# A Fourier mixing and low-rank MLP kernel: the row shift in two parts, one step moved by a loop step, other buffers for the last outputs

## The chip, the cores and the metric

The kernel runs on one core of one Trainium2 chip. A core has TensorE (matmuls, called PE in the profile; its weight loads are PEld), VectorE (DVE), ScalarE (ACT), GpSimd (POOL) and SyncE (SP), and 16 DMA engines. Each engine works through its own instructions in order; between engines, semaphores set the order. The metric is the time on the device in microseconds (us), from launch to end of one execution; lower is better.

## The reference

The input x is 8 batches of 3136 rows of 256 floats. A Fourier transform goes along the rows and along the columns, of which the real part is kept; then a low-rank mixing over the rows, and a two-layer perceptron over the columns:

```python
X = np.fft.fft(x, axis=1)
X = np.fft.fft(X, axis=2)
x = X.real.astype(np.float32)

xt = x.transpose(0, 2, 1)
h = xt @ U @ V                       # U: 3136 x 32, V: 32 x 3136
u = x + h.transpose(0, 2, 1)
ch = np.maximum(u @ w_ch1, 0.0) @ w_ch2   # 256 -> 1024 -> 256
return (u + ch).astype(np.float32)
```

## The kernel before

The 3136 rows are split as 49 x 64 (`N1`, `N2`), so that the transform along the rows becomes a small transform of 49, a turn of the layout, and a transform of 64 that is done as matmuls with a table `T`. By symmetry only 25 of the 49 lines (`NK1`) are needed. The low-rank step is folded in: the lower 64 partitions of `g` hold the turned data, the upper 64 hold the low-rank vector `te` spread over all 25 lines, and the upper half of `T` holds V.

The work has three stretches:

**The front** (to about 31 us), written out by hand: tables of sines are built, the weights folded, and batch 0 transformed alone. `x_round` runs the transform of 49 for some of the 32 columns of each quarter (`quarter_products`, line 227, into PSUM), and evacuates them into `zts[0]` (columns 0 to 15) or `zts[1]` (16 to 31). `quarter_rows` (line 229) then shifts rows: eight copies, two for each of four groups of 32 partitions, bring a `zts` tile into `g0`. For `zts[1]` (line 669) six are on VectorE and two on ScalarE; in the profile they are copies `g<-zt` of 32x800 or 31x800 at the helper lines 76 and 73. Then follow `te_single` (line 293: 50 matmuls at line 298, two copies of the result to `te` at 269 and 270, and a `spread` of `te` over `g`), and the first groups of `s3_steps`.

**The loop** (from line 821) goes over 4 pairs of batches, in chunks of 512 rows at most, and each chunk has four loop steps. A step runs `mlp1` of this chunk (line 383: four matmuls into the PSUM tile `hps`, evacuated at 385 by ScalarE as `hT`), `mlp2` of the chunk before (394 and 397), then what `plan` has placed at this step, and last `drain`, the output of finished rows. `plan` (line 780) writes the order out by step numbers: `place(steps, lo, hi)` spreads a list of steps evenly over the loop steps from lo to hi. The first pair has in its list:

- `turned_steps` of batch 1, steps 10 to 17: as in the front, eight matmul rounds with `copy_act` into `zt`, and after every second one a `quarter_rows` of eight VectorE copies of 32x400, the last of them in step 17;
- `te_single` of batch 1 at step 18, with `spread_pool`: three GpSimd copies (line 306) over the lines 0 to 8, 9 to 16, and 17 to 24;
- the thirteen groups of `s3_steps` of batch 1 (line 322: matmuls of `T` and `g`, evacuated into `q`), over steps 19 to 30, evacuated by `copy_dve`;
- `place_next`: the loads of the next pair in eight chunks, at intervals of 2.6 steps from step 8: a load on SyncE (`xa`, line 96) and a gather on GpSimd (`xb`, line 99); four steps later the fold on GpSimd (144); seven later the fold on VectorE (134 to 136); nine and ten later two groups of `s1_steps` (matmuls at 185, evacuated by ScalarE into `z`).

`teps`, `tps` and `ps` of all these come in turn from one PSUM pool of two buffers (`psd`).

**The tail**: after the last chunk's `mlp1` steps, four calls of `mlp2` with `last` set are left. Each has a `drain` of its own: ScalarE copies half of the PSUM tile to `om` (406), VectorE adds and subtracts into `ob` (407, 408), and two DMAs store it (412). `ob` is from `opool`, which has four buffers, so a drain waits for the stores of the fourth drain before it.

Of the kernel before, what the change touches and what calls it, by code (L numbers as in the profile page):

```python
# [8 lines left out]
BF16 = mybir.dt.bfloat16  # L9
FP16 = mybir.dt.float16  # L10
FP32 = mybir.dt.float32
# [7 lines left out]
N1, N2, NK1 = 49, 64, 25  # L19
# [3 lines left out]
def kernel(  # L23
# [10 lines left out]
    B, S, D = x.shape  # L34
    R = moe_U.shape[1]
    H = moe_w_ch1.shape[1]
    P = 128
# [191 lines left out]
    def quarter_rows(g, zt, i0, engines):  # L229

        n = zt.shape[4]
        for q in range(4):
            d0 = 32 * q + i0
            for c in range(2):
                r = 32 - c
                engines[2 * q + c](g[32 * c:32 * c + r].rearrange("p k (s d) -> p k s d", s=2)[:, :, :, d0:d0 + n],
                                   zt[32 * q:32 * q + r, c])
# [55 lines left out]
    def te_single(pr, b, spread, ps=None):  # L293

        ps = ps or psd.tile([P, 2, D], FP32, tag="ps", name="teps")
        for k in range(NK1):
            for s, cs in enumerate([slice(0, 129), slice(129, 256)]):
                nc.tensor.matmul(ps[32 * s:32 * s + 32, 0, cs], us[:, k, s::2], pr.g[b][0:64, k, cs],  # L298
                                 start=(k == 0), stop=(k == NK1 - 1))
        te_out(pr, b, ps, 0, 32, spread)  # L300
# [13 lines left out]
    def s3_steps(pr, b, evac):  # L314

        if pr.q is None:
            pr.q = qpool[pr.p % 2].tile([P, 2, 6272], BF16, tag="q", name="q")

        def mm(o, k1, blk, st, rows=P, low=None):
            lt = low[:, blk::2] if low is not None else pr.g[b][0:rows, k1, blk::2]  # L320
            r = T[0:rows, k1, 0:64] if k1 == 0 else T[0:rows, k1, :].rearrange("p (s j) -> p s j", s=2)
            nc.tensor.matmul(o, lt, r, start=st, stop=True, skip_group_check=True)  # L322

        def lines(ps, g, blk, rows, low=None):
            for u in range(4):
                us = slice(u * 64, (u + 1) * 64)
                mm(ps[:, 0, us] if 4 * g + u == 0 else ps[:, :, us], 4 * g + u, blk, u == 0 and low is None, rows, low)

        def step(g, blk):
            ps = psd.tile([P, 2, 256], FP32, tag="ps", name="ps")  # L330
            lines(ps, g, blk, P)
            move(ps, g, blk, evac)

        def move_part(ps, g, blk, evac, part):
            lo = 64 if part and g == 0 else 0
            c0 = 3200 + b * 1536 + (4 * g - 1) * 64 if part else b * 1600 + 4 * g * 64
            evac(pr.q[:, blk, c0 + lo:c0 + 256], ps[:, part, lo:256])

        def move(ps, g, blk, evac):
            if g == 0:  # L340
                move_part(ps, g, blk, evac, 0)
                move_part(ps, g, blk, evac, 1)
            else:
                k0 = 4 * g
                evac(two(pr.q[:, blk, :], b * 1600 + k0 * 64, 3200 + b * 1536 + (k0 - 1) * 64, 256), ps[:])

        def last():
            ps = psd.tile([P, 2, 2, 64], FP32, tag="ps", name="ps")
            k1 = NK1 - 1
            for blk in range(2):  # L350
                mm(ps[:, blk], k1, blk, blk == 0)
            for blk in range(2):
                evac(two(pr.q[:, blk, :], b * 1600 + k1 * 64, 3200 + b * 1536 + (k1 - 1) * 64, 64), ps[:, blk])

        yield lines, move_part
        for g in range(6):
            for blk in range(2):
                yield lambda g=g, blk=blk: step(g, blk)
        yield last
# [27 lines left out]
    def mlp2(ch, t, last=False):  # L387
        q, nt = ch.pr.q, len(ch.units) // 2
        if t % 2 == 0 or last:
            ch.po = pso.tile([P, 2, 2, P], FP32, tag="o", name="ops")  # L390
        ps = ch.po[:, 0 if last else t % 2]
        tk = slice(ch.c0 + t * P, ch.c0 + (t + 1) * P)
        for j in range(JT):
            nc.tensor.matmul(ps, ch.h[:, j, t * P:(t + 1) * P], W2[:, j, :],  # L394
                             start=(j == 0 and (t % 2 == 0 or last)), stop=(j == JT - 1), skip_group_check=True)
            if j < 2:
                nc.tensor.matmul(ps[:, j], q[:, j, tk], (Bp if ch.sg > 0 else Bm)[:, j], start=False, stop=False,  # L397
                                 skip_group_check=True)
        if not (last or t % 2 == 1 or t == nt - 1):
            return lambda: None  # L400

        def drain():
            n = 1 if last else t % 2 + 1
            ob = opool.tile([P, 2, D], FP32, tag="ob", name="ob")
            om = opool.tile([P, 2, P], FP32, tag="om", bufs=2, name="om")
            nc.scalar.copy(om[:, 0:n], ch.po[:, 0:n, 1])  # L406
            nc.vector.tensor_tensor(ob[:, 0:n, 0:P], ch.po[:, 0:n, 0], om[:, 0:n], op=AL.add)  # L407
            nc.vector.tensor_tensor(ob[:, 0:n, P:D], ch.po[:, 0:n, 0], om[:, 0:n], op=AL.subtract)  # L408

            def store(i, hf, engine):  # L410
                b, r0 = ch.units[2 * (t - n + 1 + i) + hf]
                engine.dma_start(out=out[b].rearrange("(k2 k1) d -> k1 k2 d", k1=N1)[r0],  # L412
                                 in_=ob[hf * 64:(hf + 1) * 64, i])

            if not last or t == 0:
                for i in range(n):
                    for hf in range(2):
                        store(i, hf, nc.sync)
            else:
                store(0, 0, nc.sync)  # L420
                late.append(lambda: store(0, 1, nc.scalar))
            while last and late and (t == 1 or t == nt - 1):
                late.pop(0)()
        return drain
# [110 lines left out]
    def w2_fold(i):  # L535
        nc.vector.tensor_tensor(W2[:, :, i * P:(i + 1) * P], w2_f[:, :, 0], w2_f[:, :, 1],
                                op=(AL.subtract if i else AL.add))

    zts = [kpool.tile([P, 64 * NK1], BF16, name=f"zt{i}", tag=f"zt{i}").rearrange(
        "p (c k s i) -> p c k s i", c=2, k=NK1, s=2) for i in range(2)]  # L540
    g1 = gpool.tile([P, NK1, D], BF16, tag="g1", name="w2_f")
    w2_f = g1[:, 0:16].bitcast(FP32).rearrange("p (t s) d -> p t s d", s=2)

# [95 lines left out]
    def x_round(ps, i0, n):  # L639
        quarter_products(X0, ps, i0, n)  # L640

        def out(evac):
            j = i0 % 16
            evac(zts[i0 // 16][:, :, :, :, j:j + n].rearrange("p c k s i -> p s c k i"),
                 ps[:, :, :, :, 0:NK1].rearrange("p i s c k -> p s c k i"))
        return out

# [18 lines left out]
    outs = [x_round(round_view(bank_o("tps")), 24 + 4 * i, 4) for i in range(2)]  # L666
    outs[0](copy_act)
    outs[1](copy_act)
    quarter_rows(g0, zts[1], 16, [copy_dve] * 6 + [copy_act] * 2)
    nc.vector.tensor_copy(T[0:64, :, 64:128], T[0:64, :, 63::-1])  # L670

    teps = bank2("teps")
# [107 lines left out]
    def plan(p):  # L780

        at = [[] for _ in range(NS)]

        def place(steps, lo, hi):
            steps = list(steps)
            for i, s in enumerate(steps):
                at[lo + i * (hi - lo) // len(steps)].append(s)

        def place_next(nx, a, gap, s3lo):

            s1 = list(s1_steps(nx, copy_act))
            for c, (load, fn, fd) in enumerate(load_steps(nx)):
                for o, f in [(0, load), (4, fn), (7, fd), (9, s1[2 * c]), (10, s1[2 * c + 1])]:
                    at[int(a + gap * c) + o].append(f)
            e = int(a + gap * 7) + 11
            place([lambda: (turn(nx, 0, [(0, 8), (8, NK1)]), turn(nx, 1, whole))], e, e + 1)
            place(te_steps(nx, spread_pool), e, e + 2)
            place(list(s3_steps(nx, 0, copy_dve))[1:], s3lo, NS)

        cur = pairs[p]  # L800
        if p == 0:
            rest = []
            for t, f in zip([1, 2, 2, 3, 4, 5, 5, 6, 8], s3b0[4:]):
                at[t].append(f)
            at[0].append(lambda: w2_fold(0))
            at[2].append(lambda: w2_fold(1))
            place([late_tables], 8, 9)
            place([load_uz], 24, 25)
            place([lambda: rest.append(pair_tables())], 6, 7)
            place([lambda: rest[0]()], 10, 11)  # L810
            place(turned_steps(cur, 1, X1), 10, 18)
            place([lambda: te_single(cur, 1, spread_pool)], 18, 19)
            place(list(s3_steps(cur, 1, copy_dve))[1:], 19, 31)
            place_next(pairs[1], 8, 2.6, 44)
        else:
            place(list(s3_steps(cur, 1, copy_dve))[1:], 3, 18)
            if p + 1 < NP:
                place_next(pairs[p + 1], 0, 3.4, 40)
        return at
# [50 lines left out]
```

## The time and the profile before

Six runs gave a median of 451.67 us (450.75 to 453.93). The profiled execution took 454.93 us, with a span of 453.1 us from its first instruction to its last; the rest lies around it.

| what | us | share of the span |
|---|---|---|
| TensorE busy | 428.2 | 94% |
| ScalarE busy | 290.5 | 64% |
| VectorE busy | 226.0 | 50% |
| GpSimd busy | 142.9 | 32% |
| granted TensorE clock, mean | 0.990 of full | |

A row of the profile's tables reads: source line, engine, operation, output from input with their shapes, number of instructions, busy time, mean time of one, and then the idle time of that engine before it, with what ended the idle time behind the arrow. In the timeline, the first two numbers are the start and the length in us. A row of the windows shows a stretch, its length, the busy time of TensorE, its weight loads, VectorE, ScalarE and GpSimd with their number of instructions, then the granted clock, the busy share of the DMA engines, and GB/s.

### The profile page before, as it was taken

The numbers are of one execution on the slowest core, as the hardware profiler recorded it, in microseconds if no ns is written. First come the engines' busy times: TensorE is split into PE (matmuls) and PEld (weight loads), VectorE is DVE, ScalarE is ACT, GpSimd is POOL, SyncE is SP. The second block draws the span as 40 slices with busy tenths as digits, with TensorE's granted clock in tenths as the row PEclk, the third lists the DMA queues.
The fourth block names the chain that finished last, engine by engine and source line by source line (L and its number), as shares of the span: only waits on it lengthen the run. The fifth ranks groups of instructions, "written<-read, shape, count | busy, mean of one in ns | idle before, by whom it ended". The sixth has DMA issues, their size and how long they took to land.

```text
span 453.1 us, 10536 instructions
## 1 busy us (share of the span) xinstructions
PE 428.2 (94%) x4158; PEld 309.9 (68%) x4221; DVE 226.0 (50%) x541; ACT 290.5 (64%) x402; POOL 142.9 (32%) x180
## 2 busy tenths in 40 slices
PE   3699998999999999999999999999999999999995
PEld 1566665677867777767767777667767777677763
DVE  7674586766336367663354366663355345112212
ACT  5587754677465666777466666777465665666662
POOL 7445464951150544660420443660410000000000
PEclk9999998999999999999999999999999999999999
DMA  8749753785492538663682547763662222222323
GB/s 144 158 140 138 201 175 96 241 212 176 130 253 66 163 111 244 219 191 116 165 206 71 146 125 243 221 194 112 163 141 71 71 60 65 73 74 71 84 58 93
DMA packets 59761, 64.34 MB, mean 142 GB/s; under 512 B 12950, under 2 KB 52672, under 8 KB 59552
## 3 DMA queue, kind: packets, MB, share of 16 engines
q1 hardware_dynamic: 50000, 42.68, 35.9%
q0 software_dynamic: 7232, 14.30, 13.1%
q10 hardware_dynamic: 2480, 6.69, 3.9%
q8 instruction: 33, 0.54, 0.5%
q14 instruction: 16, 0.13, 0.1%
HBM read 34.62 MB, written 32.19 MB: 147 GB/s over the span
## 4 chain that ended last, share of the span: by engine, by line
PE 86%; DMA 4%; DVE 3%; issue 2%; SPq 1%; ACT 1%; POOL 1%; DVEq 0%; POOLq 0%
PE ops L394 36%; PE hps L383 35%; PE ps L322 5%; PE ops L397 5%; PE ps L185 3%; DMA X<-in_x_dram 2%; DMA out_dram<-ob 2%; PE tps L227 1%; DVE g L76 1%; PE teps L284 1%; SPq L412 1%; PE teps L298 1%; ACT hT L385 1%; DVE q L76 0%; DVE ob L407 0%
## 5 line engine op out<-in xcount | busy, mean ns | idle before, releaser
L385 ACT ACTIVATE hT<-hps 128x1024 bf16<-128x1024 f32 (+1 forms) x208 | 202.4, 975 | 111.0 <-PE hps L383 103.9
L394 PE MATMUL ops<-W,hT 128*128 128x256 bf16 x1568 | 225.2, 273 | 1.0 <-DVE ob L408 0.7
L394 PEld LDWEIGHTS <-hT 128*128 128x128 bf16 x1568 | 145.4, 98 | 35.3 <-DVE ob L408 0.8
L76 DVE CAST q<-ps 128x512 bf16<-128x512 f32 (+3 forms) x121 | 65.2, 559 | 85.7 <-PE ps L322 81.5
L383 PE MATMUL hps<-q,W1p 128*128 128x512 bf16 (+1 forms) x420 | 103.2, 355 | 2.3 <-DVE q L76 0.5
L407 DVE TENSOR_TENSOR ob<-ops,om 128x256 f32<-128x256 f32 (+1 forms) x102 | 41.8, 409 | 114.7 <-ACT om L406 113.9
L383 PE MATMUL hps<-q,W1m 128*128 128x512 bf16 x351 | 96.4, 381 | 2.2 <-ACT hT L385 0.5
L144 POOL TENSOR_TENSOR y<-xa,xb 98x510 f32<-98x510 f32 (+1 forms) x48 | 61.5, 1301 | 106.3 <-DMA xa<-in_x_dram 90.4
L383 PEld LDWEIGHTS <-W1p 128*128 128x128 bf16 x448 | 40.3, 97 | 26.9 <-issue 1.7
L383 PEld LDWEIGHTS <-W1m 128*128 128x128 bf16 x384 | 35.5, 98 | 26.9 <-issue 2.0
L397 PEld LDWEIGHTS <-q 128*128 128x128 bf16 x392 | 38.5, 98 | 21.5 <-issue 1.0
L406 ACT COPY om<-ops 128x256 f32<-128x256 f32 (+1 forms) x102 | 37.2, 365 | 12.5 <-PE ops L394 7.9
L306 POOL COPY g<-te 64x1024 int32<-64x1024 int32 (+1 forms) x23 | 24.8, 1120 | 60.9 <-DVE te L270 56.3
L408 DVE TENSOR_TENSOR ob<-ops,om 128x256 f32<-128x256 f32 (+1 forms) x102 | 41.0, 402 | 0.0
L73 ACT CAST z<-ps 128x512 bf16<-128x512 f32 x48 | 28.1, 585 | 17.9 <-PE ps L185 16.1
L397 PE MATMUL ops<-Bp,q 128*128 128x128 f16 x200 | 38.4, 219 | 0.0
L322 PE MATMUL ps<-T,g 128*128 128x128 bf16 (+3 forms) x400 | 36.9, 218 | 0.3 <-ACT q L73 0.3
L397 PE MATMUL ops<-Bm,q 128*128 128x128 f16 x192 | 37.1, 220 | 0.0
L322 PEld LDWEIGHTS <-g 128*128 128x128 bf16 (+1 forms) x400 | 29.5, 98 | 4.5 <-DVE q L76 0.4
L99 POOL DMA_INDIRECT xb<-in_x_dram,idx x24 | 24.4, 1018 | 5.4 <-issue 4.4
L76 DVE COPY g<-zt 32x400 bf16<-32x400 bf16 (+3 forms) x45 | 17.2, 382 | 8.7 <-ACT zt L73 8.1
L135 DVE TENSOR_TENSOR yb<-y 98x508 bf16<-98x508 f32 (+1 forms) x24 | 20.7, 862 | 0.0
(136 smaller groups left out, 211.3 us busy)
## 6 DMA issues: line engine op xcount, KB each, us to landing
out_dram<-ob SPq DMA_DIRECT2D x389, 64.0 KB
xa<-in_x_dram SPq DMA_DIRECT2D x24, 392.0 KB
zturn<-z ACTq DMA_DIRECT2D x9, 512.0 KB
g<-zturn SPq DMA_DIRECT2D x3, 800.0 KB
g<-zturn SPq DMA_DIRECT2D x3, 544.0 KB
X<-in_x_dram POOLq DMA_DIRECT2D x4, 384.0 KB, 8.5
X<-in_x_dram POOLq DMA_DIRECT2D x2, 744.0 KB
zturn<-z ACTq DMA_DIRECT2D x3, 448.0 KB
```

The lines of the kernel that those rows point to most:

```text
L73: nc.scalar.copy(o, i)
L76: nc.vector.tensor_copy(o, i)
L144: nc.gpsimd.tensor_tensor(ck.y[:, l0:l1, 1:256], ck.xa[:, l0:l1, 1:256], rb[:, l0:l1, 255:0:-1], op=AL.add)
L306: eng.tensor_copy(g[64:128, k0:k1].bitcast(I32), src.unsqueeze(1).to_broadcast([64, k1 - k0, D // 2]))
L322: nc.tensor.matmul(o, lt, r, start=st, stop=True, skip_group_check=True)
L383: nc.tensor.matmul(ps[:, i, 0:n], (W1p if ch.sg > 0 else W1m)[jp // 2][:, blk, j], q[:, blk, c0:c0 + n], start=(blk == 0), stop=(blk == 1))
L385: nc.scalar.activation(ch.h[:, 2 * jp:2 * jp + 2, 0:n], ps[:, :, 0:n], AF.Relu)
L394: nc.tensor.matmul(ps, ch.h[:, j, t * P:(t + 1) * P], W2[:, j, :], start=(j == 0 and (t % 2 == 0 or last)), stop=(j == JT - 1), skip_group ...
L397: nc.tensor.matmul(ps[:, j], q[:, j, tk], (Bp if ch.sg > 0 else Bm)[:, j], start=False, stop=False, skip_group_check=True)
L406: nc.scalar.copy(om[:, 0:n], ch.po[:, 0:n, 1])
L407: nc.vector.tensor_tensor(ob[:, 0:n, 0:P], ch.po[:, 0:n, 0], om[:, 0:n], op=AL.add)
L408: nc.vector.tensor_tensor(ob[:, 0:n, P:D], ch.po[:, 0:n, 0], om[:, 0:n], op=AL.subtract)
```

## The change

There are three edits. First, the second half of batch 0's columns gets two tiles of 8 columns each, `zts[1]` and `zts[2]`, in place of one of 16, and `quarter_rows` is called once for each, with six copies on VectorE and two on ScalarE each time. Second, in `plan`, `te_single` of batch 1 goes from step 18 to step 19, its thirteen groups of `s3_steps` go over steps 20 to 30, and these are evacuated by `copy_alt` (line 80), which alternates between ScalarE and VectorE. Third, `ob` of the last chunk's drains is taken from `xpool` under the tag `xa`, whose four buffers hold the input chunks earlier on.

```diff
         def drain():
             n = 1 if last else t % 2 + 1
-            ob = opool.tile([P, 2, D], FP32, tag="ob", name="ob")
+            ob = (xpool.tile([P, 2, D], FP32, tag="xa", name="ob") if last else
+                  opool.tile([P, 2, D], FP32, tag="ob", name="ob"))
...
-    zts = [kpool.tile([P, 64 * NK1], BF16, name=f"zt{i}", tag=f"zt{i}").rearrange(
-        "p (c k s i) -> p c k s i", c=2, k=NK1, s=2) for i in range(2)]
+    zts = [kpool.tile([P, 4 * n * NK1], BF16, name=f"zt{i}", tag=f"zt{i}").rearrange(
+        "p (c k s i) -> p c k s i", c=2, k=NK1, s=2) for i, n in enumerate([16, 8, 8])]
...
         def out(evac):
             j = i0 % 16
-            evac(zts[i0 // 16][:, :, :, :, j:j + n].rearrange("p c k s i -> p s c k i"),
+            zt = zts[0][:, :, :, :, j:j + n] if i0 < 16 else zts[i0 // 8 - 1][:, :, :, :, j % 8:j % 8 + n]
+            evac(zt.rearrange("p c k s i -> p s c k i"),
                  ps[:, :, :, :, 0:NK1].rearrange("p i s c k -> p s c k i"))
...
-    quarter_rows(g0, zts[1], 16, [copy_dve] * 6 + [copy_act] * 2)
+    for i in range(2):
+        quarter_rows(g0, zts[1 + i], 16 + 8 * i, [copy_dve] * 6 + [copy_act] * 2)
...
-            place([lambda: te_single(cur, 1, spread_pool)], 18, 19)
-            place(list(s3_steps(cur, 1, copy_dve))[1:], 19, 31)
+            place([lambda: te_single(cur, 1, spread_pool)], 19, 20)
+            place(list(s3_steps(cur, 1, copy_alt))[1:], 20, 31)
```

## The prediction

> **What bounds the kernel now.** I read the page's busy shares first, then the chain of waits, then what TensorE waited for, and last the timeline and the windows around the longest of those waits.
>
> ```profile
> PE 428.2 (94%) x4158; PEld 309.9 (68%) x4221; DVE 226.0 (50%) x541; ACT 290.5 (64%) x402; POOL 142.9 (32%) x180
> PE 86%; DMA 4%; DVE 3%; issue 2%; SPq 1%; ACT 1%; POOL 1%; DVEq 0%; POOLq 0%
> ```
>
> TensorE is busy 94% of the 453.1 us and carries 86% of the chain. So only what leaves TensorE idle or slow, or what comes after its last matmul, can move the time. The waits of TensorE between 20 and 100 us name the place:
>
> ```profile
> PE tps L227 <- issue: 2.9, 2, 2.5
> PE teps L298 <- DVE g L76: 1.5, 1, 1.5
> PE ps L185 <- DVE q L76: 0.6, 1, 0.6
> ```
>
> The columns are total us, times, longest. The second row is the low-rank step of batch 1 waiting for VectorE's last eight row copies. The timeline there:
>
> ```profile
> 70.91 1.27 POOL L144 TENSOR_TENSOR y<-xa,xb 98x510 f32<-98x510 f32 x1
> 71.13 3.04 DVE L76 COPY g<-zt 32x400 bf16<-32x400 bf16 x8 [0.90 <-ACT zt L73]
> ...
> 74.22 1.73 PE L298 MATMUL teps<-g,us 64*32 64x129 bf16 x50 [1.48 <-DVE g L76]
> ...
> 76.96 3.12 POOL L306 COPY g<-te 64x1152 int32<-64x1152 int32 x3 [4.60 <-issue]
> ```
>
> The copies end at 74.17; TensorE, done with its multilayer work at 72.74, stands 1.48. The windows show a second cost (the granted clock is the number before the DMA share):
>
> ```profile
> 72.00:74.00 2.00, 0.74 (x8) 0.41 (x5) 1.90 (x8) 0.81 (x1) 0.36 (x2) 1.00 0.39 98
> 74.00:76.00 2.00, 1.78 (x51) 1.58 (x52) 1.97 (x6) 0.00 (x0) 0.00 (x0) 0.88 0.03 8
> 76.00:78.00 2.00, 1.78 (x6) 0.77 (x7) 0.79 (x3) 0.59 (x1) 1.04 (x1) 0.50 0.13 33
> 78.00:80.00 2.00, 2.00 (x19) 1.58 (x17) 0.16 (x1) 1.02 (x1) 2.00 (x3) 0.76 0.46 115
> ```
>
> After the stall the clock falls to 0.50 until about 79.
>
> **Part 1, the first batch's row shift.** Six VectorE copies of 32x800 become twelve of 32x400; two ScalarE copies become four. VectorE stands still for 2.39 before 23.62, waiting for the last ScalarE copy of the transform. With own buffers its first six copies need only the first of those, begun at 21.71 and 0.83 long: they start at 22.56. Eight back-to-back copies of 32x400 took 2.12 at 66.08, so 0.265 each; twelve make 3.18 and end at 25.74, against 25.83 now. The table's median of 0.255 agrees; its mean of 0.38 holds the few copies that ran against a GpSimd fold, and GpSimd is idle from 22.07 to 28.24. TensorE ends its weight products (24.54 and 1.29) at 25.83 and starts the low-rank step at 25.89. So at most 0.06 is won.
>
> ScalarE pays. A 31x800 copy takes 0.855; half the elements take between half of it (0.43) and, by the 0.49 of a 128x400 evacuation, 0.52. Four make 1.7 to 2.1 against 1.72: 0 to 0.4 later. Behind them in ScalarE's queue stand two copies into T, W1p, Bp and the first q copies, which end at 30.29; the first hidden-layer matmul runs at 30.20, straight behind the second weight fold (29.18, 1.18 long), which hides most of the shift. I book 0 (from -0.06 to +0.4).
>
> **Part 2, the low-rank step a loop step later.** Removed from its place: 50 matmuls, two te copies on VectorE, three spread copies on GpSimd. In between now come the second matmul pair of chunk 0 (0.22) and one step of multilayer work (1.85, start to start, as at 436.17 to 438.02). TensorE: 72.74 + 0.22 + 1.85 = 74.81, later than 74.17, so the stall of 1.48 goes. The step's 50 matmuls took 1.59 at 25.89 near full clock, but the one here began before the clock fell and took 1.73: I use 1.5 to 1.6, ending at 76.4.
>
> The clock. From 75.88 to 79.34 the chunk pair and one step took 3.46, against 0.23 + 1.85 = 2.08 for the same at full clock (80.59 to 82.67): 1.38 lost. Here a rule speaks against me. The Trainium skill, TensorE: Matmul & The Clock Gate, HAM oscillation, says that idle gaps above some 3.4 us throttle the array; 1.48 is far less. By the rule alone the slow stretch is not the stall's and stays, so the part saves 1.5; by the row, where the only long stall of this stretch is followed by 0.50, it saves about 2.9. The same page's Part 1 calls the window free-running, so a short gap may or may not count. I take the row. Its 1.38 is the least certain term, since an unprofiled run may lie differently to the window.
>
> What is late next. The te copies follow the 50 matmuls; in the trace GpSimd starts its spread 1.01 after they end (75.95 to 76.96), so at about 77.4. Its first copy of three (3.12 / 3 = 1.04) ends at 78.4. TensorE, after the pair of chunk 1 (0.22) and another step (1.85), is at 78.4 to 78.5: a wait of 0 to 0.1.
>
> The queues that the move passes. On GpSimd the gather of chunk 4 (a DMA issue of 0.97) now stands before the spread. The order of the changed program shows that the spread's first copy also waits for that gather's landing, as it waits for the one of chunk 3 now. Free at 72.37, GpSimd issues it at about 72.4. Landings in the trace took 3.8 (issued 80.38, at a low DMA share) up to 7.9 (51, at a share of 0.71 to 0.90). At 72 to 76 the share is 0.39, then 0.03, so I take 3.8: 76.2, ahead of te. At 7.9 it is 80.3 and costs 2.9 (rival B). A second rule bears on it: the skill's SBUF — State Buffer, "SBUF: two separate sides", says that a VectorE copy in a two-port mode keeps GpSimd from writing a gather's descriptors. Then the landing counts from the copies' end: 74.2 + 3.8 = 78.0, and 0.6 is lost. The gather at 63.54 ran within such copies (60.76 to 65.37) in 0.97, the same as the median 0.96, so I go with 76.2. SyncE's order is unchanged; its load of chunk 4 already precedes. VectorE's te copies stay behind the stores' additions of the step before, which end at 76.22: no loss.
>
> The evacuations. Of batch 1's thirteen groups, about half move from VectorE to ScalarE. After the first two groups TensorE waits 0.59 for four VectorE copies in a row (79.84 to 81.12); with two engines I work out 0.45, since ScalarE reaches them only after the hidden layer's activation: 0.14 gained. Six copies of 512 columns (0.58) and two or three small ones load ScalarE by some 4 us between 78 and 106, on 23.97 busy of 34 (78 to 112): about 80%. Activations have two PSUM buffers and follow their matmuls by a step, so a delay of half a microsecond is covered; if not, 0.5. The thirteen groups now share eleven steps instead of twelve, but the first chunk that reads batch 1 (step 24) still finds its groups done by step 22.
>
> Sum: 1.48 + 1.38 + 0.14, and 0.1 back for the te matmuls at the better clock, less 0.1 for the spread: **3.0 saved**. TensorE stays busy (33.2 of 34 us from 78 to 112), so it passes to the end; SyncE's backlog behind the UZ load at 94.23 starts with stores that move along with TensorE.
>
> **Part 3, the last output buffers.** VectorE's last addition waits 0.47 for a store, and starts 0.60 after its ScalarE copy where the two before start after 0.30: 0.3 seems to be won. But the end hangs on SyncE:
>
> ```profile
> 441.81 8.78 SPq L412 DMA_DIRECT2D out_dram<-ob  x12
> L412 SPq DMA_DIRECT2D out_dram<-ob x1: 546/546/546, 450.0 to 450.0; - x1
> ```
>
> It issues stores without a pause from 445.0 to 450.55; the last data are ready at 449.44, the last store starts at 450.0. The 0.3 is hidden: 0 (from -0.3 to 0).
>
> **Sum and time.** The profiled run took 454.93 (span 453.1); less 3.0 it is 451.9. It stands 3.3 above the median of 451.67 (450.75 to 453.93), so I carry the difference: 451.67 - 3.0 = **448.7**.
>
> **The rivals.** 0.5% is 2.3 us, about what a measurement can tell from no change.
> - A, chance 0.60: as summed, 447.7 to 449.4.
> - C, 0.27: the stall goes but the slow clock was not in most runs, or comes anyway: 1.48 + 0.14 less 0.1 = 1.5, so 450.2 (449.4 to 450.9). For it: the other runs lie below the profiled one, and the rule above. Against: the windows.
> - B, 0.07, the other side: the gather of chunk 4 holds the spread. From a landing at 77.4 on, each microsecond is one of TensorE's. At 7.9 the spread starts at 80.3 and its first copy ends at 81.4: 2.9 idle, and if the clock falls again as it does now, 1.4 more. Net 3.0 - 4.3: 453.0, slower than before by 0.3%. It breaks even at about 6.6 from issue to landing. For it: two landings of 7.8 and 7.9. Against: the quiet DMA.
> - D, 0.06: ScalarE is too full, in front (0.4) and with thirteen groups (0.5 to 1), with small stalls that bring the slow clock (1.4): 450.4 to 453, and a tenth of it beyond.
>
> The range 447.6 to 451.6 leaves out the far parts of A, B and D. Faster by over 0.5% (under 449.4): A and a little of D, 0.62. Within: C, the middle of B and D, 0.33. Slower: the ends of B and D, 0.05.
>
> **What would show it.** Right: no wait of the 50 matmuls on the row copies, the clock at 1.00 from 72 to 80, the spread starting about a microsecond after the matmuls, the wait of 0.6 shortened, the low-rank step of batch 0 still at 25.9, SyncE still issuing to the end. Wrong: a wait of TensorE on the spread or of the spread on the gather, ScalarE copies ahead of a hidden-layer wait, or a low clock that stays.

## The result and the profile after

The changed kernel takes a median of **451.91 us** (449.6 to 453.77, 34 runs); the kernel before, beside it on the same chip, 452.73 (71 runs). The ratio is 0.998, with a 95% interval of 0.9967 to 0.9992: some 0.8 us faster, where 3.0 were forecast. A second comparison gave 0.9994 (0.9974 to 1.0014). No more than half a microsecond to one is there. Here and below, a ratio and its interval are worked out from all runs of both kernels, so a ratio need not equal the quotient of the two medians beside it.

The profiled execution took 451.8, with a span of 450.0. That is 3.1 less than the profiled execution before, and so very nearly the forecast. The median did not follow. Explaining this gap is most of what comes below.

The first two lines are the busy shares and the chain of waits of the kernel after:

```profile
PE 426.0 (95%) x4159; PEld 308.5 (69%) x4221; DVE 223.9 (50%) x539; ACT 294.4 (65%) x412; POOL 143.8 (32%) x180
PE 88%; DVE 6%; ACT 2%; issue 2%; POOL 0%; DVEq 0%; POOLq 0%; ACTq 0%
```

TensorE is busy 2.2 us less than before although it has the same work: it ran fewer microseconds at half clock. ScalarE has 3.9 us more, mostly the evacuations that it took over. Next, what TensorE waited for between 20 and 100 us (in total, times, longest):

```profile
PE teps L298 <- DVE g L76: 0.8, 1, 0.8
PE ps L185 <- DVE q L76: 0.7, 1, 0.7
...
PE ps L185 <- ACT q L73: 0.5, 1, 0.5
```

The first row looks like the old stall, halved. It isn't: its place is 23.93, in the front, where batch 0's low-rank step waits for the split row shift. The stall of batch 1 is gone, as the timeline from 68 to 78 shows:

```profile
69.38 3.23 DVE L76 COPY g<-zt 32x400 bf16<-32x400 bf16 x8 [0.91 <-ACT zt L73]
...
70.78 0.95 POOL L99 DMA_INDIRECT xb<-in_x_dram,idx  x1 [0.17 <-issue]
...
73.00 1.59 PE L298 MATMUL teps<-g,us 64*32 64x129 bf16 x50
...
75.42 3.12 POOL L306 COPY g<-te 64x1152 int32<-64x1152 int32 x3 [3.68 <-DVE te L270]
...
76.61 0.57 PE L322 MATMUL ps<-T,g 128*128 128x64 bf16 x8
...
77.02 0.65 ACT L73 CAST q<-ps 128x256 bf16<-128x256 f32 x2 [0.18 <-PE ps L322]
...
77.42 0.63 DVE L76 CAST q<-ps 128x192 bf16<-128x192 f32 x2 [0.82 <-ACT q L73]
...
77.83 0.38 PE L185 MATMUL ps<-yb,F 98*128 98x258 bf16 x2 [0.66 <-DVE q L76]
```

The copies end at 72.61, the 50 matmuls start at 73.00 with no idle time named before them, and the spread starts 0.83 after they end (74.59). The gather issued at 70.78 landed 3.9 later, ahead of `te`. The first two groups at 76.61 don't wait for the spread. In the last three rows a new order shows: ScalarE and VectorE evacuate the two groups, but one after the other (VectorE waits 0.82 for ScalarE), and TensorE waits 0.66. The windows show the clock (the number before the DMA share) at full speed:

```profile
72.00:74.00 2.00, 2.00 (x47) 1.72 (x47) 1.94 (x7) 1.02 (x1) 0.00 (x0) 1.00 0.62 193
74.00:76.00 2.00, 1.94 (x32) 1.37 (x28) 1.40 (x6) 1.05 (x3) 0.58 (x1) 1.00 0.13 34
76.00:78.00 2.00, 1.34 (x18) 1.04 (x16) 1.18 (x5) 1.49 (x3) 2.00 (x3) 1.00 0.37 93
```

To see where the 3.1 us of the two profiles came from, I set the hidden-layer activations (line 385) of both side by side, 208 in each, and took the difference of their starts, after less before:

| activation | start after less before, us | reading |
|---|---|---|
| first | -1.96 | the front of before's profile ran late, partly at half clock |
| 18th | -1.75 | nothing gained yet in the loop |
| 22nd | -5.08 | 3.3 gained around the low-rank step |
| 27th | -4.01 | 0.9 given back from the 25th (-4.93) on |
| 69th | -2.98 | 1.0 given back since the 68th (-4.01), near 175 us |
| end of span | -3.1 | |

So the step that was forecast to save 3.0 did save it in this pair of profiles (3.1, once a group of 0.22 is counted that after still owes there). But 2 us of the difference is the front, where the forecast had booked nothing, and 2 us were given back later.

The late front of before's profile comes and goes. TensorE waits there once for 2.5 before a run of transform matmuls (line 227), for nothing that the profile names: it is the longest wait of the first row in the prediction's list. This wait is 2.5 to 2.9 in five of the 17 profiles (before, the repeated change and three others) and at most 1.4 in the rest, and half clock begins near its end in those five alone. In the sixteen profiles that have it, TensorE goes on 2.3 to 2.8 after a 16-KB packet of the instruction queue (q8) starts, which is at 18.1 to 18.3 in the five and at 15.7 to 16.5 in the others. Why it starts later in some is open.

### The profile page after: what moved, and what is told of

Read it like the earlier page. It is cut to its first block, busy times and chain, and to the rows that moved or that the text cites. A ratio compares the mean times of both kernels' runs of the same rounds, so it can differ in the third digit from the quotient of the medians.

```text
span 450.0 us, 10537 instructions
## 1 busy us (share of the span) xinstructions
PE 426.0 (95%) x4159; PEld 308.5 (69%) x4221; DVE 223.9 (50%) x539; ACT 294.4 (65%) x412; POOL 143.8 (32%) x180
## 4 chain that ended last, share of the span: by engine, by line
PE 88%; DVE 6%; ACT 2%; issue 2%; POOL 0%; DVEq 0%; POOLq 0%; ACTq 0%
PE ops L394 37%; PE hps L383 35%; PE ps L322 5%; PE ops L397 5%; PE ps L185 3%; DVE g L76 2%; PE tps L227 2%; PE teps L284 1%; ACT hT L385 1%; PE teps L298 1%; DVE q L76 1%; DVE ta L448 0%; DVE yb L134 0%; DVE yb L135 0%; ACT q L73 0%
## 5 line engine op out<-in xcount | busy, mean ns | idle before, releaser
L76 DVE CAST q<-ps 128x512 bf16<-128x512 f32 (+3 forms) x113 | 60.8, 558 | 84.7 <-PE ps L322 79.4
L134 DVE TENSOR_TENSOR yb<-y 98x508 bf16<-98x508 f32 (+1 forms) x24 | 21.9, 912 | 0.1
L135 DVE TENSOR_TENSOR yb<-y 98x508 bf16<-98x508 f32 (+1 forms) x24 | 21.8, 910 | 0.0
```

The lines of the kernel that those rows point to most:

```text
L76: nc.vector.tensor_copy(o, i)
```

## The experiments

Two theories to begin with. **Stall and clock**: the stall and the half clock behind it are what the move wins, and something else takes most of it back. **Clock by chance**: the half clock is not the stall's, so only 1.5 was there to win. Later runs ask what takes it back: the front, the packing of thirteen groups in eleven steps, or the wait near 175 us.

### One part at a time

**Move alone**, with the evacuations left on VectorE:

```diff
-            place([lambda: te_single(cur, 1, spread_pool)], 18, 19)
-            place(list(s3_steps(cur, 1, copy_dve))[1:], 19, 31)
+            place([lambda: te_single(cur, 1, spread_pool)], 19, 20)
+            place(list(s3_steps(cur, 1, copy_dve))[1:], 20, 31)
```

> Only the low-rank step of batch 1 goes to step 19, its groups to steps 20 to 30, evacuated by VectorE alone as before. Theory A (the stall of 1.5 us goes in every run, but the half-clock stretch followed it only in some runs, and the other parts are nothing): the same 0.8 to 1.5 us under the kernel before as the whole change. Theory B (the move saves its 3.0 us in most runs, and the evacuations on ScalarE or the front give 2 us back): 2.5 to 3 us under.

451.38 against 452.63; ratio 0.9984 (0.996 to 1.0008): about what the whole change wins, within the noise. The stall is gone, and between 68 and 100 us TensorE waits four times for an evacuation: 0.6, 0.2, 0.5 and 0.6.

**Evacuations alone**, with the step left where it was:

```diff
-            place(list(s3_steps(cur, 1, copy_dve))[1:], 19, 31)
+            place(list(s3_steps(cur, 1, copy_alt))[1:], 19, 31)
```

> Only the evacuations of batch 1's groups alternate between ScalarE and VectorE; the low-rank step stays at step 18. Theory A: within 0.3 us of the kernel before. Theory B, if ScalarE is what gives back: 1 to 2 us slower.

452.92; ratio 1.0002 (0.998 to 1.0025): nothing. The wait after the first groups is 0.7, not shorter than 0.6. The stall of 1.5 is there, but in this profile no half clock follows it.

**Front alone**, the row shift in two parts:

```diff
-    quarter_rows(g0, zts[1], 16, [copy_dve] * 6 + [copy_act] * 2)
+    for i in range(2):
+        quarter_rows(g0, zts[1 + i], 16 + 8 * i, [copy_dve] * 6 + [copy_act] * 2)
```

> Only the row shift of batch 0 in two parts. Theory A: within 0.3 us, and the low-rank step of batch 0 starts as soon after its weight products as before. Theory B, if the front gives back: 1 to 2 us slower, seen as a wait of the low-rank step on the row copies.

452.95; ratio 1.0014 (0.9995 to 1.0034). Again the stall is there and no half clock. Here are the windows of this run, and below them those of the kernel before, profiled a second time in a later run (its label is e12_before_again):

```profile
68.00:70.00 2.00, 2.00 (x16) 1.20 (x14) 1.54 (x3) 2.00 (x4) 1.66 (x3) 1.00 0.59 203
70.00:72.00 2.00, 0.52 (x19) 0.48 (x20) 1.90 (x7) 0.11 (x1) 0.00 (x0) 1.00 0.24 64
72.00:74.00 2.00, 2.00 (x46) 1.51 (x41) 1.96 (x7) 0.53 (x1) 0.00 (x0) 1.00 0.04 8
```

```profile
70.00:72.00 2.00, 1.21 (x44) 1.22 (x46) 1.94 (x6) 0.00 (x0) 0.00 (x0) 1.00 0.11 30
72.00:74.00 2.00, 2.00 (x20) 0.99 (x15) 1.37 (x6) 0.59 (x1) 0.47 (x1) 0.60 0.02 4
74.00:76.00 2.00, 2.00 (x12) 1.34 (x11) 0.00 (x0) 1.02 (x1) 2.00 (x3) 0.54 0.41 107
```

The same stall, 1.48 of idle in each, and the clock drops behind one and not behind the other. Of the six profiles that have the stall (before twice, and four experiments) two show the drop.

What sets these two apart can be read from the traces. In all 17, the recorded changes of the clock lie whole multiples of 3.41 us apart (10.24, 51.2 and 61.44, for example), as if TensorE were judged in windows of this length; where they begin differs from one profile to the next. Here is the window that holds most of the stall, and what TensorE did in it beside the low-rank step's small matmuls:

| profile | window, us | other matmuls, us | clock in the next window |
|---|---|---|---|
| before | 72.12 to 75.53 | 0.62 | 0.50 |
| before, again | 69.00 to 72.41 | 0.33 | 0.50 |
| later pairs' evacuations (below) | 73.04 to 76.46 | 0.82 | 1.00 |
| front alone, again (below) | 72.83 to 76.24 | 0.97 | 1.00 |
| front alone | 68.38 to 71.79 | 1.66 | 1.00 |
| evacuations alone | 68.16 to 71.57 | 1.97 | 1.00 |

The clock drops where the stall and most of the 50 small matmuls (64 rows, 32 columns) fall into one window, and not where the window's edges part them or more of other work lies inside. These are six cases that came by chance, not a test; what a small matmul counts for they don't settle.

**Stall filled** with six matmuls of 512 columns, whose result is overwritten by the step's own, so that TensorE is busy while it waits:

```diff
+        for i in range(6):
+            nc.tensor.matmul(ps.rearrange("p a d -> p (a d)"), W2[:, 0, 0:P], W1p[0][:, 0],
+                             start=True, stop=True)
```

> The kernel before, with six extra matmuls of 128x512 (1.3 us at full clock) that fill TensorE while it waits for the last row copies of batch 1; their result is overwritten. The stall stays as long, but the clock has no reason to fall. Theory A: the half-clock stretch is there in some runs only, so the median falls by 0.5 us or less. Theory B: it is there in most runs, and the median falls by 1 to 1.4 us.

452.33; ratio 1.0006 (0.998 to 1.0032). The six take the place of the idle time, so what is left to win is the clock alone, and it can't be seen in the median. If each execution lost 1.38 to it, the ratio would be 0.997, outside the interval.

### How often the clock drops

The profiles are few, but every run records its mean granted clock. A stretch of 3.41 us at half clock lowers the mean over 452 us by 3.41 x 0.5 / 452 = 0.0038. Counting a mean below 0.9965 as one such stretch, below 0.9925 as two, below 0.9885 as three, gives what the traces of all 17 profiled executions show. Over all runs for which a clock is on record (the filled stall is among those without; ± is one standard error):

| kernels | runs | share with a stretch | stretches per run |
|---|---|---|---|
| with the stall, front as before | 282 | 49% | 0.61 ± 0.04 |
| with the stall, front split | 36 | 53% | 0.94 ± 0.19 |
| without the stall, front as before | 86 | 30% | 0.35 ± 0.06 |
| without the stall, front split | 115 | 52% | 0.68 ± 0.07 |

The stall brings 0.26 stretches a run, not one, and the split front brings 0.33. (Set against runs on the same chip alone, they bring 0.23 ± 0.08 and 0.34 ± 0.09.) Runs of the kernel before with no stretch average 451.73, with one 452.92: a stretch costs about 1.2. So the stall's clock is worth 0.26 x 1.2, some 0.3 us, and the split loses about 0.4 by the same sum.

### The thirteen groups

Packing thirteen groups in eleven steps pairs two of them at step 25 as well. The timeline of the kernel after:

```profile
89.08 0.61 PE L322 MATMUL ps<-T,g 128*128 128x128 bf16 x8
...
89.51 0.59 ACT L73 CAST q<-ps 128x512 bf16<-128x512 f32 x1 [0.18 <-PE ps L322]
...
90.14 0.38 PE L185 MATMUL ps<-yb,F 98*128 98x258 bf16 x2 [0.45 <-ACT q L73]
```

Eight matmuls back to back fill both buffers of the pool, and the next product waits 0.45 for an evacuation. Before had no such wait. Three runs change the packing: the change with the groups over twelve steps; the change with the pairs placed by hand; and that placement without the front split and the tail.

```diff
-            place(list(s3_steps(cur, 1, copy_alt))[1:], 20, 31)
+            place(list(s3_steps(cur, 1, copy_alt))[1:], 20, 32)
```

> The changed kernel, its thirteen groups of batch 1 over twelve steps (20 to 31) instead of eleven, so that only step 20 has two groups and no longer step 25. Theory A (the new waits of TensorE for evacuations, 0.66 us after the pair of step 20 and 0.45 us after the pair of step 25, eat what the stall gave): the wait of 0.45 us is gone from the trace, and the median lies 0.4 to 0.5 us under the changed kernel. Rival R (the folds of VectorE and GpSimd, which now fall together, slow everything behind them, whatever the places of the groups): no difference from the changed kernel.

```diff
-            place(list(s3_steps(cur, 1, copy_alt))[1:], 20, 31)
+            for t, f in zip([20, 21, 21, 22, 23, 24, 25, 26, 27, 28, 29, 30, 31],
+                            list(s3_steps(cur, 1, copy_alt))[1:]):
+                at[t].append(f)
```

> The changed kernel with the thirteen groups placed by hand at steps 20, 21, 21, 22, 23 and so on to 31: the one pair stands in step 21, where no transform matmuls of the next pair follow it. Theory A: both waits of TensorE for evacuations are gone, and the median lies 0.9 to 1.1 us under the changed kernel. Rival R: no difference.

> The changed kernel again, to be compared with the others on the same chip and to see a second profile of it. Theory A: 0.8 us under the kernel before; the waits for evacuations of about 0.7 and 0.5 us stand in its trace again, the one of 1.05 us near 175 us may not. Rival R: the wait near 175 us stands again.

> The kernel before with only the low-rank step at step 19 and the groups of batch 1 placed as in the last but one run, alternating between ScalarE and VectorE; the row shift of batch 0 and the last output buffers as before. Theory A (front and tail edits give nothing): as the run with both, within 0.3 us. If the front's edit costs: 0.3 us or more below it.

All against 452.34. Over twelve steps: 451.17, 0.9987 (0.9968 to 1.0005); the 0.45 is gone and 0.7 at step 20 stays. By hand: 451.46, 0.9988 (0.9972 to 1.0003); both are gone, but a wait of 0.9 on a VectorE evacuation takes their place. The change again: 452.59, 0.9994. By hand without the split and the tail: 450.72, 0.997 (0.9953 to 0.9987), in spite of the same 0.9. The two kernels placed by hand differ by 0.7 in the median; that points to the front, though they differ in the tail's buffers as well.

### The wait near 175 us, and a version that beats both

The repeated change shows what gave a microsecond back near 175 us:

```profile
174.01 3.20 POOL L144 TENSOR_TENSOR y<-xa,xb 98x510 f32<-98x510 f32 x2 [4.21 <-DMA xa<-in_x_dram]
...
174.32 1.76 DVE L135 TENSOR_TENSOR yb<-y 98x508 bf16<-98x508 f32 x1
...
176.00 1.25 DVE L136 CAST yb<-y 98x8 bf16<-98x8 f32 x1
...
177.81 1.27 DVE L76 CAST q<-ps 128x512 bf16<-128x512 f32 x2
...
178.54 0.38 PE L185 MATMUL ps<-yb,F 98*128 98x258 bf16 x2 [1.10 <-DVE q L76]
```

A fold on VectorE that takes 0.68 elsewhere takes 1.76 while GpSimd folds, and a copy of 8 columns 1.25 instead of 0.17. The evacuations queue behind them. Is this the change's? The kernel before, profiled again, answers: between 110 and 180 us it has the same wait.

```profile
PE ps L185 <- DVE q L76: 1.1, 1, 1.1
```

It comes and goes with where the folds meet. Before had it in one of two profiles, after in both, and the experiments in some: in six of all 13 profiles in which VectorE alone evacuates the later pairs. The next runs evacuate the later pairs' groups on both engines in turn, so that nothing queues behind a fold alone:

```diff
-            place(list(s3_steps(cur, 1, copy_dve))[1:], 3, 18)
+            place(list(s3_steps(cur, 1, copy_alt))[1:], 3, 18)
```

First it is put on top of the placement by hand, without split and tail, with that placement alone and the kernel before once more beside it:

> The kernel before with the low-rank step at step 19 and the groups of batch 1 placed without a pair ahead of transform matmuls, and in the later pairs the groups of the second batch evacuated by ScalarE and VectorE in turn instead of VectorE alone. Theory A2 (VectorE's folds, held up while GpSimd folds, delay the evacuations queued behind them, and TensorE waits 1.05 us for one near 175 us): that wait is gone or under 0.5 us, and the median is 0.3 to 1 us below the run with VectorE alone. Rival (that wait is chance and seldom): no difference, or slower by what ScalarE adds.

> The kernel before with only the low-rank step at step 19 and the groups of batch 1 placed without a pair, once more: 1.0 to 1.6 us under the kernel before if the first result holds. A2: a wait of TensorE of about 1 us for VectorE near 170 to 180 us stands in its trace again. Rival: it does not.

> The kernel before, for a second profile. Theory A (the half-clock stretch after the stall is rare, and the rest of its profiled run's excess lay in the front): the stall of 1.5 us stands, the clock stays full after it. Theory B: half clock for 3.4 us after the stall again. A2 as a part of the change: no wait of 1 us near 175 us here. Rival: one may stand here too.

449.06 against 451.82, ratio **0.9944** (0.9928 to 0.9959); without the later pairs' edit 450.19, 0.9973 (0.995 to 0.9995); before against itself 0.9998 (0.9982 to 1.0013). In the first of these, TensorE's only wait between 110 and 180 us is 0.2:

```profile
PE hps L383 <- ACT hT L385: 0.2, 1, 0.2
```

Then the same again with the front split, without it, the later pairs' edit alone, and the front split alone:

> The best version so far (low-rank step at step 19, no pair of groups ahead of transform matmuls, later pairs evacuated by ScalarE and VectorE in turn) with the row shift of batch 0 in two parts added. Theory F (the split costs in the front: more and longer copies there, and more half-clock windows): 0.4 to 0.6 us slower than the same kernel without the split, and a lower mean clock over its runs. Rival (the split is nothing): within 0.2 us.

> The best version once more, beside the one with the split on the same chip: 2 to 3 us under the kernel before if its first 7 runs hold; no wait of about 1 us near 175 us.

> The kernel before with only the later pairs' groups evacuated by ScalarE and VectorE in turn; the stall at the low-rank step of batch 1 stays. A2 (the wait of about 1 us near 175 us is in the kernel before too, in most runs): about 1 us under the kernel before. Rival (the wait came with the change): no difference.

> The kernel before with only the row shift of batch 0 in two parts, once more. Theory F: 0.4 to 0.6 us slower than the kernel before. Rival: within 0.2 us.

Against 453.39: with the split 450.91, 0.9944 (0.992 to 0.9968); without it **449.81, 0.9932** (0.9908 to 0.9956); the later pairs' edit alone 452.01, 0.9974 (0.9957 to 0.999); the split alone 453.98, 1.0027 (1.0001 to 1.0052). The version without the split, with the low-rank step at 19, the groups placed by hand and both engines evacuating all pairs, beats the kernel before in both of its comparisons; the change was not beside it there, but its ratios (0.998 and 0.9994) lie above both intervals. The 1.1 between the medians with and without the split fits the front's cost, though the intervals overlap. The wait near 175 us stands in none of the four profiles with the later pairs' edit. That accounts for some 0.5 on average (1.1 in six of 13), while the edit alone won 1.2; what else it wins is open.

What the split does in the front is read from two timelines. With it (the kernel after):

```profile
19.64 1.62 ACT L73 CAST zt<-tps 128x800 bf16<-128x800 f32 x3 [0.66 <-PE tps L227]
...
20.50 3.37 DVE L76 COPY g<-zt 32x400 bf16<-32x400 bf16 x12
...
21.14 2.12 ACT L73 COPY g<-zt 32x400 bf16<-32x400 bf16 x4
...
23.93 1.59 PE L298 MATMUL teps<-g,us 64*32 64x129 bf16 x50 [0.84 <-DVE g L76]
```

Without it (the best version, second run):

```profile
19.50 1.62 ACT L73 CAST zt<-tps 128x800 bf16<-128x800 f32 x3 [0.35 <-PE tps L227]
...
21.15 2.21 DVE L76 COPY g<-zt 32x800 bf16<-32x800 bf16 x6 [0.54 <-ACT zt L73]
...
23.41 1.59 PE L298 MATMUL teps<-g,us 64*32 64x129 bf16 x50 [0.33 <-DVE g L76]
```

Counted from the start of ScalarE's evacuations, the twelve copies start 0.79 earlier (0.86 against 1.65) and take 1.16 longer (3.37 against 2.21; 0.28 each against 0.37). From the end of the transform's matmuls to the low-rank step, in the profiles at full clock there, it is 3.36 to 3.70 in the six with the split. In the six without it is 2.98 to 2.99 four times, and 3.26 and 3.65 in the filled stall and the kernel before, again. On average that is about 0.4 later (3.5 against 3.1). In three of the six with the split a stretch of half clock follows, in none of the six without; the split alone, second run:

```profile
26.00:28.00 2.00, 2.00 (x22) 1.80 (x21) 0.54 (x2) 0.84 (x2) 1.28 (x2) 0.50 0.93 327
28.00:30.00 2.00, 2.00 (x16) 1.90 (x14) 0.85 (x2) 1.24 (x4) 1.95 (x2) 0.50 0.04 10
```

The edit of the last output buffers had no run of its own; the two traces settle it (below).

## Why the prediction was wrong

The direction was right, the size was not: 3.0 forecast, 0.8 measured, and the range just missed the median. By its own steps:

- **The stall of 1.48: right.** The 50 matmuls start without idle time. The gather's landing (3.8 taken, 3.9 measured), the start of the spread (1.01 taken, 0.83 measured) and the queues it passes were right as well. Rival B did not happen.
- **The half clock, 1.38: mis-sized, the main miss.** It was booked in full from one trace, against the rule that the prediction weighed (the Trainium skill, TensorE: Matmul & The Clock Gate, HAM oscillation). Neither the row nor the rule alone holds. Half clock follows the gap of 1.48 in two of six profiles, which a rule of gaps above 3.4 doesn't allow; but mostly it does not. The runs show 0.26 stretches per execution at about 1.2, so some 0.3; rival C had said that the slow clock was not in most runs. The free-running window of the page's Part 1 fits this and the six windows above: the same idle time counts or does not by where it lies. No run moved the window on purpose.
- **The profile's own excess, carried as a constant: the same mistake seen from the other side.** The profiled execution stood 3.3 above the median because of a slow front and the half clock. Part of what the change removed in the profile was that excess, which the median never had. The prediction took 3.0 off both.
- **The first batch's row shift, booked at 0 (up to +0.4): wrong, and a loss.** The lead of 1.06 for VectorE's copies came from a front at half clock (20.92 to 24.33 in before's profile), in which ScalarE's evacuations stood apart:

```profile
21.71 1.22 ACT L73 CAST zt<-tps 128x800 bf16<-128x800 f32 x2 [1.94 <-PE tps L227]
...
23.10 0.49 ACT L73 CAST zt<-tps 128x400 bf16<-128x400 f32 x1 [0.17 <-PE tps L227]
...
23.62 2.21 DVE L76 COPY g<-zt 32x800 bf16<-32x800 bf16 x6 [2.39 <-ACT zt L73]
```

  In the profiles at full clock there they run back to back in 1.62, and the lead is 0.79 in the kernel after. There, too, TensorE mostly stands idle before the low-rank step without the split (0.1 to 0.9 in five of six), so these copies are what it waits for, and the 0.06 that the prediction read held for a late TensorE alone. The cost of a split copy was nearly right (0.265 taken, 0.28 measured). So it costs about 0.4 at the low-rank step and, by the runs' clocks, about 0.4 more; the two runs of this edit alone stand 0.14% and 0.27% above the kernel before (0.6 and 1.2 us), the first not apart from nothing by its interval. Rival D named this place, but with ScalarE as the late engine; the step waits for VectorE.
- **The evacuations, 0.14 won: wrong sign.** In each of the two groups VectorE's copy starts only when ScalarE's has ended (77.42 after 77.39, 77.70 after 77.67), so the wait went from 0.59 to 0.66. Thirteen groups in eleven steps were given no cost; they brought a second pair and 0.45. Of the 0.9 given back there, 0.45 is this wait and 0.22 the group owed; the rest I did not trace.
- **The tail, 0: right.** In the kernel after VectorE's last addition waits 0.17, for its ScalarE copy and no longer for a store (0.47 before):

```profile
445.50 0.29 DVE L408 TENSOR_TENSOR ob<-ops,om 128x128 f32<-128x128 f32 x1 [0.17 <-ACT om L407]
```

  Yet from the start of the last hidden-layer activation to the end of the span it is the same 10.4 before (442.78 to 453.1) and after (439.63 to 450.0): the last data are ready at 445.99, and SyncE starts the last store at 446.88.

The sum redone: 1.48 won by the stall and some 0.3 by the clock; 0.07 and 0.45 lost to evacuations, and twice about 0.4 to the front. This leaves some 0.5 won, beside 0.8 and 0.3 in the two comparisons. The wait of 1.1 near 175 us can blur this. That the change makes it likelier is not shown, since before has it too.

## What to carry to other kernels

A loss that one profile shows is worth its size times how often it happens: compare the profiled execution's time and mean clock with those of the other runs before a slow stretch is booked in full. Where a profile stands above the median, part of what is to be won in it does not exist in the median. When groups of work are packed into fewer steps, count which of them now stand back to back, and how many buffers they share: two buffers and two groups in a row cost a wait here, whichever engines evacuate.

## What the runs showed that was not expected

- A stall of 1.48 us is followed by 3.41 us at half clock in some profiles and not in others, and the six cases part by how it lies to a fixed grid of 3.41 us. Over the runs of one program such a stretch makes a difference of about 1.2 us.
- The folds of VectorE and GpSimd hold one another up. Near 174 us above, GpSimd's two take 3.20 instead of 2.50. In the kernel after, a VectorE fold of 0.68 takes 3.17 beside two of GpSimd's:

```profile
83.08 3.17 DVE L134 TENSOR_TENSOR yb<-y 98x508 bf16<-98x508 f32 x1
83.20 2.50 POOL L144 TENSOR_TENSOR y<-xa,xb 98x510 f32<-98x510 f32 x2
```

  It ends 0.55 after GpSimd's pair, within one fold's own length. The Trainium skill, SBUF — State Buffer, section "SBUF: two separate sides", says that a VectorE operation with two inputs in SBUF and a GpSimd operation that reads SBUF hold a shared port for a whole instruction each, which agrees with this row. The page also gives the port to whichever starts first; by the starts in this trace that was VectorE's fold, by 0.12, and yet it was the one that waited. In this kernel it matters through the evacuations that queue behind such a fold.
